# Routed attention with a two-layer feed-forward: two key transfers, the centroids' scaling and their turned copy handed to ScalarE

## The chip, the cores and the metric

The kernel runs on one core of a Trainium2 chip. The metric is the device time of one execution in microseconds (us); lower is better. Each timing below is the median of several executions of the same program.

The core has five engines that work side by side, each through its own list of instructions: TensorE (PE, with weight loads as PEld), VectorE (DVE), ScalarE (ACT), GpSimd (POOL) and SyncE (SP). SP and ACT also issue the DMA transfers of this kernel's prologue; "SPq" and "ACTq" in the profile are such issues.

## What is computed

A routed attention, and a feed-forward behind it. Every query and key is assigned to the centroid to which it is most alike, and a query sees only the keys with the same centroid as itself.

```python
q, k, v: (4, 8, 768, 64)      centroids: (8, 16, 64)
q_n, k_n, c_n = each vector divided by (its norm + 1e-06)
q_assign = argmax over the 16 centroids of q_n . c_n        # k_assign likewise
mask = q_assign[:, :, :, None] == k_assign[:, :, None, :]
scores = where(mask, q k^T / 8, -1e9)
attn = softmax(scores);  x = (attn v), as (3072, 512)
h = x @ w_in                                                # (3072, 2048)
out = (h * erf(softplus(h))) @ w_out                        # (3072, 512)
```

The centroids' scaling `c_n = centroids / (norm + 1e-6)` is the part of this that the change touches; it is done once, for all eight heads.

## The kernel before

The attention works on 16 pairs of heads (`NPAIR`), one after the other. The first two pairs are prepared by straight-line code, the *prologue*; then `period(p, i)` is called six times for each pair and mixes the work of three pairs: the attention of one, the masks of the next and the loads of the one behind it. After the pairs comes the feed-forward (products in banks named `bank`), which is more than half of the time. All of the engines' work up to there is emitted through `InOrder`, a small wrapper that keeps every instruction in the order in which it stands in the program on its engine. So nothing is rescheduled: an instruction that waits holds up all that stand behind it on the same engine.

The prologue, in the order in which the program emits it:

1. **Loads.** `load(p, nm, src, pl)` brings q or k of one pair in four transfers of 96 KB, one for each head `e` of the pair and each half `g` of the 64 features. `queues` holds SP at place 0 and ScalarE at place 1. Of the first pair's q, head 0 goes by SP and head 1 by ScalarE; of its k, `queues[e * g]` sends only the fourth transfer by ScalarE and three by SP. The centroids (32 KB) go by SP ahead of everything. Behind ScalarE's two q transfers stands the load of its function table (`preload_act_table_set`, line 253), and behind that its k transfer. From line 255 on all transfers go by SP: q and k of the second pair (into `x_more`), later those of the third (`load_qk(2)`, line 1498).
2. **Centroids.** Lines 346 to 368. The 128 centroids lie one to a partition in `cen`, a strip of the buffer `pr` (so these steps carry the name `pr` in the profile). VectorE squares and sums them (355, 356), bounds the sum from below (357), ScalarE makes the root through logarithm and exponential (359, 360), VectorE refines it by one Newton step and takes the reciprocal (361 to 367), and then writes the scaled centroids twice side by side into `cn` (368).
3. **Warm-up.** `warm(n, bank, rhs)` (line 1479) issues n matmuls whose results nobody reads: 17 with 256 columns (line 1484), then the one that turns `cn` into the bank `pct` (1486), then 3 with 384 columns (1487). `turned` is the name of both banks in the profile.
4. **Turning.** VectorE turns q into `qT` (1490), copies the two halves of `pct` into `ccT` (1491 to 1495), and turns k into `kT` (1496).
5. **Routing of the first pair.** `similarities(0)`: TensorE multiplies `ccT` with `qT` and `kT`; ScalarE casts `qT` and `kT` to bf16 (`vectors`, tiles `qv` and `kv`); VectorE fills `pick` (lines 1502 to 1509); TensorE does `products(0)` and 9 more warm-up matmuls (1512); `choose(0)` on VectorE turns the similarities (`sims`), takes the maximum (`wide`), compares (`hot`) and turns back (`hotT`). The matmuls of `masks` need `hotT`, and everything after needs the masks.

Of the kernel before, what the change touches and what calls it, by code (L numbers as in the profile page):

```python
# [9 lines left out]
F32 = mybir.dt.float32  # L10
# [5 lines left out]
ACT = mybir.ActivationFunctionType  # L16
# [3 lines left out]
P = 128  # L20
# [115 lines left out]
def kernel(  # L136
# [13 lines left out]
    te, ve, ae, ge = (  # L150
        InOrder(tc, e, in_order) for e in (nc.tensor, nc.vector, nc.scalar, nc.gpsimd)
    )

    def pool(name, bufs, **kw):
        return ctx.enter_context(tc.tile_pool(name=name, bufs=bufs, **kw))

    const = pool("const", 1)
# [3 lines left out]
    turned = [ps.tile([P, 512], F32, name=f"turned{i}") for i in range(2)]  # L161
# [5 lines left out]
    x_more = const.tile([P, 3, HK, HT], F32, name="x_more")  # L167
    minus = const.tile([P, Q], F32, name="minus")
    alleps = const.tile([P, 1], F32, name="alleps")
    x_dram = dram.tile([DM, B * S], F32, name="x_dram")  # L170

    attention = ctx.enter_context(ExitStack())

    def passing(name, bufs, **kw):
        return attention.enter_context(tc.tile_pool(name=name, bufs=bufs, **kw))
# [4 lines left out]
    const = passing("fixed", 1)  # L180
# [8 lines left out]
    pick = const.tile([P, 2, P], BF16, name="pick")  # L189
# [25 lines left out]
    queues = [sy, ae]  # L215

    def heads(p):
        return p // HP, 2 * (p % HP)

    def load(p, nm, src, pl):  # L220
        if p >= NPAIR:
            return
        b, h0 = heads(p)
        if nm == "v":
            t = pl.tile([P, NJ, 2, D], F32, name="in_v")
            for e in range(2):
                queues[0].dma_start(out=t[:, :, e], in_=src[b, h0 + e].rearrange("(j p) d -> p j d", p=P))
        else:

            if pl is None:  # L230
                t = x_more.rearrange("p a k t -> p (a k t)")[:, (nm == "k") * S : (1 + (nm == "k")) * S]
                t = t.rearrange("p (n t) -> p n t", t=Q)
            else:
                t = pl.tile([P, NB, Q], F32, name="in_" + nm)
            for e in range(2):
                for g in range(D // Q):
                    queues[e if nm == "q" else e * g].dma_start(
                        out=t[e * D + g * Q : e * D + (g + 1) * Q],
                        in_=src[b, h0 + e, :, g * Q : (g + 1) * Q].rearrange("(n t) d -> t n d", t=Q),
                    )  # L240
        pairs.setdefault(p, {})[nm] = t

    def load_qk(p):
        load(p, "q", q, stage if p != 1 else None)
        load(p, "k", k, stage if p != 1 else None)
# [3 lines left out]
    cen = setup[:, 0:D]  # L249
    sy.dma_start(out=cen, in_=centroids.rearrange("h c d -> (h c) d"))  # L250

    load(0, "q", q, stage)
    tc.keep_in_program_order(nc.scalar.preload_act_table_set("natural_log_exp_and_others"))
    load(0, "k", k, stage)
# [9 lines left out]
    for base, pattern, sign, op, fill in (  # L264
# [5 lines left out]
            out=first, in_=first, compare_op=op, fill=fill, base=base, pattern=pattern,  # L270
# [69 lines left out]
    ve.tensor_copy(out=identb, in_=ident)  # L340
    ve.memset(minus, -1.0)
    ve.memset(alleps, S * EPS)
    for t in lowest + least:
        ge.memset(t, 0.0)

    cn = setup[:, D : 3 * D].rearrange("p (e d) -> p e d", e=2)
    spare = iter(range(TW, HW))

    def scalar_tile():
        n = next(spare)  # L350
        return setup[:, n : n + 1]

    sq = cn[:, 0]
    ss = scalar_tile()
    ve.tensor_tensor(out=sq, in0=cen, in1=cen, op=ALU.mult)
    ve.reduce_sum(out=ss, in_=sq, axis=AX.X)
    ve.tensor_scalar_max(out=ss, in0=ss, scalar1=1e-30)
    norm = scalar_tile()
    ae.activation(out=norm, in_=ss, func=ACT.Ln)
    ae.activation(out=norm, in_=norm, func=ACT.Exp, scale=0.5)  # L360
    inv = scalar_tile()
    ve.reciprocal(out=inv, in_=norm)
# [2 lines left out]
    norm = scalar_tile()  # L365
    ve.tensor_scalar(out=norm, in0=twice, scalar1=0.5, scalar2=1e-6, op0=ALU.mult, op1=ALU.add)
    rden = scalar_tile()
    ve.reciprocal(out=rden, in_=norm)
    for e in range(2):
        ve.tensor_scalar_mul(out=cn[:, e], in0=cen, scalar1=rden)  # L370

    def transposes(p, which="qk"):

# [1105 lines left out]
    def warm(n, bank, rhs):  # L1479
        for _ in range(n):  # L1480
            te.matmul(bank[:, 0 : rhs.shape[-1]], lhsT=identb, rhs=rhs, start=True, stop=True)

    zeros = lowest[1].rearrange("p t n -> p (t n)")
    warm(17, turned[1], pick.rearrange("p h n -> p (h n)"))
    pct = turned[0][:, 0:P]
    te.transpose(out=pct, in_=cn.rearrange("p e d -> p (e d)"), identity=ident)
    warm(3, turned[1], zeros)
# [1 line left out]
    st["qT"], st["kT"] = rows[0]["q"], rows[0]["k"]  # L1489
    ve.transpose(out=st["qT"], in_=st.pop("q").rearrange("p n t -> p (n t)"))  # L1490
    for e in range(2):
        ve.tensor_copy(
            out=ccT[e * D : (e + 1) * D, :, e * C : (e + 1) * C],
            in_=pct[e * D : (e + 1) * D].rearrange("d (r e c) -> d r e c", e=2, c=C)[:, :, e],
        )
# [6 lines left out]
    for r in (0, D):  # L1502
        for half in range(2):
            for e in range(2):
                c = r + half * Q + e * C
                ve.tensor_copy(
                    out=pick[r : r + D, half, e * D : (e + 1) * D].rearrange("p (n c) -> p n c", n=2)[:, :, 1 : C + 1],
                    in_=first[r : r + D, c : c + C].unsqueeze(1).to_broadcast([D, 2, C]),
# [137 lines left out]
```

## Time and profile before

| | |
|---|---|
| time, median of 3 runs | 950.37 us (950.34 to 950.56) |
| the profiled execution's own time | 950.65 us |
| its span, first to last instruction | 948.9 us |
| TensorE busy | 939.7 us, 99% of the span |
| VectorE, ScalarE, GpSimd busy | 789.1, 546.5, 504.6 us |
| prologue up to the first mask matmul | the first 11.31 us of the span |

A row of the timeline reads: start and duration in us, engine, line, operation, what it writes <- what it reads, shapes, how many instructions are merged in the row, and in brackets how long the engine had been idle before and what it waited for. Since every operation is recorded in the wrapper, nearly all rows name its line, L127; the tiles tell which step it is. In the chain of waits a row is start, duration, engine and what was at work. Matmuls overlap one another, so the time from one start to the next is the better measure of their pace than their durations.

### The profile page before, as it was taken

How to read it: one execution, taken by the hardware profiler on the slowest of the kernel's cores; microseconds unless marked ns; L12 is line 12 of the kernel's file. 1: busy time of each engine (PE TensorE's matmuls, PEld its weight loads, DVE VectorE, ACT ScalarE, POOL GpSimd, SP SyncE). 2: the span in 40 equal slices, each digit the busy share in tenths (PEclk: the TensorE clock that was granted, in tenths of full speed). 3: DMA queues.
4: the chain of work that ended last, by engine and by line, in shares of the span. 5: the costliest groups of instructions: out<-in, count | busy, mean ns of one | idle time of the engine just before them, and what ended most of it. 6: DMA issues, size and time to landing. Idle time of an engine off the chain costs nothing.

```text
span 948.9 us, 22319 instructions
## 1 busy us (share of the span) xinstructions
PE 939.7 (99%) x8756; PEld 707.2 (75%) x8756; DVE 789.1 (83%) x1417; ACT 546.5 (58%) x809; POOL 504.6 (53%) x357
## 2 busy tenths in 40 slices
PE   8999999999999999999999999999999999999998
PEld 3555555555555555588888888998999899989987
DVE  8888888888888887879886688688868977897887
ACT  3677777777777776476523643654257236525541
POOL 1688888888888888899108211360063016103600
PEclk9999999999999999999999999999999999999999
DMA  9344554444443621132876347353444336343433
GB/s 220 69 114 113 112 113 113 111 113 111 113 112 68 156 56 36 26 120 112 220 209 248 111 117 203 123 180 111 157 158 143 133 115 209 113 153 123 156 112 111
DMA packets 176344, 123.17 MB, mean 130 GB/s; under 512 B 132592, under 2 KB 143344, under 8 KB 176240
## 3 DMA queue, kind: packets, MB, share of 16 engines
q1 hardware_dynamic: 171872, 116.34, 42.5%
q0 software_dynamic: 1872, 4.98, 2.9%
q8 instruction: 69, 1.13, 0.5%
q10 hardware_dynamic: 2496, 0.43, 0.2%
q14 instruction: 35, 0.29, 0.1%
HBM read 91.78 MB, written 23.33 MB: 121 GB/s over the span
## 4 chain that ended last, share of the span: by engine, by line
PE 93%; DVE 2%; ACT 2%; issue 1%; POOL 1%; DMA 1%; SPq 0%; DVEq 0%; POOLq 0%; ACTq 0%
PE bank L127 40%; PE turned L127 31%; PE sc L127 16%; PE wide L127 6%; POOL more_out L127 1%; DVE nmx L127 1%; DVE g L127 1%; ACT a_s L127 0%; DMA g_more<-in_moe_w_out_dram 0%; ACT L127 0%; ACT osb L127 0%; ACT w_out L127 0%; SPq L127 0%; DMA qm<-least_rows 0%; ACT g_more L127 0%
## 5 line engine op out<-in xcount | busy, mean ns | idle before, releaser
L127 POOL TENSOR_TENSOR more_out<-more_out,pr 128x768 f32<-128x768 f32 x128 | 217.6, 1700 | 17.1 <-ACT pr L127 7.5
L127 DVE TENSOR_REDUCE nmx<-wide 128x2 f32<-128x512 f32 (+2 forms) x189 | 179.1, 948 | 47.1 <-PE wide L127 46.0
L127 ACT ACTIVATE pr<-sc 128x768 f32<-128x768 f32 x192 | 148.4, 810 | 81.3 <-PE wide L127 73.3
L127 PE MATMUL turned<-pr,in_v 128*32 128x193 f32 x3072 | 145.2, 330 | 0.0
L127 POOL TENSOR_TENSOR g<-g 128x512 f32<-128x512 f32 x36 | 47.1, 1309 | 180.8 <-DVE g L127 178.9
L127 PEld LDWEIGHTS turned<-pr,in_v 128*32 128x32 f32 x3072 | 90.2, 109 | 51.3 <-issue 26.9
L127 DVE TENSOR_TENSOR g<-g 128x512 f32<-128x512 f32 x132 | 90.8, 688 | 22.3 <-PE bank L127 11.8
L127 PE MATMUL sc<-qT,kT 64*128 64x384 f32 x528 | 98.5, 485 | 0.0
L127 DVE TENSOR_TENSOR g<-bank,g 128x256 f32<-128x256 f32 (+1 forms) x128 | 64.7, 531 | 16.1 <-PE bank L127 9.5
L127 PE MATMUL bank<-g_more,g 128*128 128x256 f32 x320 | 75.7, 379 | 0.0
L127 PE MATMUL bank<-x_own,w_in 128*128 128x128 f32 (+1 forms) x440 | 74.0, 310 | 0.0
L127 ACT ACTIVATE a_s<-g 128x1024 f32<-128x1024 f32 x38 | 39.5, 1054 | 57.4 <-POOL g L127 45.6
L127 POOL TENSOR_TENSOR more_out<-pr,pr 128x768 f32<-128x768 f32 x32 | 59.1, 1848 | 20.0 <-ACT pr L127 19.9
L127 DVE TENSOR_TENSOR g<-a_s,g 128x512 f32<-128x512 f32 x76 | 68.2, 916 | 0.9 <-ACT a_s L127 0.9
L127 PEld LDWEIGHTS bank<-g_more,g 128*128 128x128 f32 x320 | 60.7, 190 | 8.6 <-DVE g L127 0.4
L127 PEld LDWEIGHTS bank<-x_own,w_in 128*128 128x128 f32 x440 | 63.1, 191 | 4.6 <-issue 0.6
L127 PE MATMUL wide<-kv,qv 64*128 64x256 bf16 (+2 forms) x378 | 64.8, 327 | 0.9 <-ACT km L127 0.6
L127 PE MATMUL bank<-w_out,g 128*128 128x256 f32 x280 | 64.5, 379 | 0.0
L127 ACT ACT_TABLE_LOAD x40 | 51.3, 1283 | 19.8 <-DVE g L127 19.2
L127 PEld LDWEIGHTS <-qv 64*128 64x128 bf16 x384 | 23.1, 93 | 52.7 <-issue 37.9
L127 PE MATMUL wide<-km,qm 64*128 64x256 bf16 (+4 forms) x378 | 62.2, 326 | 0.0
L127 PEld LDWEIGHTS sc<-qT,kT 64*128 64x128 f32 x528 | 46.3, 187 | 19.0 <-issue 2.0
(240 smaller groups left out, 1992.6 us busy)
## 6 DMA issues: line engine op xcount, KB each, us to landing
g_more<-b_dram SPq DMA_DIRECT2D x52, 512.0 KB
g_more<-w_dram SPq DMA_DIRECT2D x84, 256.0 KB
x_own<-in_moe_w_in_dram SPq DMA_DIRECT2D x13, 512.0 KB
in_v<-in_v_dram SPq DMA_DIRECT2D x32, 192.0 KB
x_dram<-more_out SPq DMA_DIRECT2D x128, 48.0 KB
x_own<-x_dram SPq DMA_DIRECT2D x6, 1024.0 KB
in_k<-in_k_dram SPq DMA_DIRECT2D x59, 96.0 KB
in_q<-in_q_dram SPq DMA_DIRECT2D x58, 96.0 KB
```

The costliest lines, as they stand in the source:

```text
L127: ins = getattr(self.engine, name)(*args, **kw)
```

## The change

- `load` sends both transfers of head 1 by ScalarE for k too, so that SP issues two of the first pair's four k transfers and ScalarE two.
- The instruction that bounds the sum of squares from below is gone; the logarithm takes 1e-30 as a bias from a new tile `tiny`, which VectorE fills once.
- The two scalings into `cn` move from VectorE to ScalarE.
- The first warm-up has 15 matmuls instead of 17.
- The two copies of `pct` into `ccT` move from VectorE to ScalarE. They keep their place in the program, ahead of the casts of `qT` and `kT`.

```diff
+    tiny = const.tile([P, 1], F32, name="tiny")
...
-                    queues[e if nm == "q" else e * g].dma_start(
+                    queues[e].dma_start(
...
     ve.memset(alleps, S * EPS)
+    ve.memset(tiny, 1e-30)
...
-    ve.tensor_scalar_max(out=ss, in0=ss, scalar1=1e-30)
     norm = scalar_tile()
-    ae.activation(out=norm, in_=ss, func=ACT.Ln)
+    ae.activation(out=norm, in_=ss, func=ACT.Ln, bias=tiny)
...
     for e in range(2):
-        ve.tensor_scalar_mul(out=cn[:, e], in0=cen, scalar1=rden)
+        ae.activation(out=cn[:, e], in_=cen, func=ACT.Identity, scale=rden)
...
-    warm(17, turned[1], pick.rearrange("p h n -> p (h n)"))
+    warm(15, turned[1], pick.rearrange("p h n -> p (h n)"))
...
     for e in range(2):
-        ve.tensor_copy(
+        ae.copy(
             out=ccT[e * D : (e + 1) * D, :, e * C : (e + 1) * C],
             in_=pct[e * D : (e + 1) * D].rearrange("d (r e c) -> d r e c", e=2, c=C)[:, :, e],
         )
```

## The prediction

> **What bounds the kernel now.** I read the page's busy times first, then the chain of waits in order of time, then the timelines of the engines over the first 14 us.
>
> ```profile
> span 948.9 us, 22319 instructions
> PE 939.7 (99%) x8756; PEld 707.2 (75%) x8756; DVE 789.1 (83%) x1417; ACT 546.5 (58%) x809; POOL 504.6 (53%) x357
> ```
>
> TensorE is busy nearly throughout, and the change touches no matmul behind the prologue. It can only move the point from which TensorE's unbroken work starts. The chain of waits over the first 40 us, and one row of the chain over the whole span:
>
> ```profile
> 2.41 4.04 PE turned L127 x18
> ...
> 6.70 0.23 DVE ccT L127
> ...
> 6.96 0.99 DVE kT L127
> ...
> 7.99 0.86 PE turned L127 x4
> 8.88 0.59 DVE sims L127
> ...
> 11.31 0.32 PE wide L127
> ```
>
> ```profile
> 404.83 3.59 DMA g_more<-in_moe_w_out_dram
> ```
>
> The prologue hangs on one thread: 18 matmuls (17 warm-ups and the turning of `cn`), the copies into `ccT`, the turning of k, the similarities of k, then VectorE's `sims` to `hotT`, then the mask matmul at 11.31. Whatever is won or lost ahead of `sims` arrives at 11.31 unchanged, if TensorE is free by then, and from there in the end: the one long transfer in the later chain, at 404.83, is issued behind work that moves along. VectorE and ScalarE in detail:
>
> ```profile
> 2.76 0.23 DVE L127 TENSOR_TENSOR pr<-pr 128x64 f32<-128x64 f32 x1 [0.37 <-DMA pr<-in_centroids_dram]
> ...
> 3.28 0.15 DVE L127 TENSOR_SCALAR pr<-pr 128x1 f32<-128x1 f32 x1
> ...
> 4.58 0.16 DVE L127 RECIPROCAL pr<-pr 128x1 f32<-128x1 f32 x1
> 4.78 0.42 DVE L127 TENSOR_SCALAR pr<-pr 128x64 f32<-128x64 f32 x2
> 5.11 0.97 DVE L127 STREAM_TRANSPOSE qT<-in_q 128x768 f32<-128x768 f32 x1
> 6.47 0.46 DVE L127 COPY ccT<-turned 64x64 f32<-64x64 f32 x2 [0.39 <-PE turned L127]
> 6.96 0.98 DVE L127 STREAM_TRANSPOSE kT<-in_k 128x768 f32<-128x768 f32 x1
> 7.86 0.79 DVE L127 COPY pick<-first 64x32 bf16<-64x32 bf16 x8
> ```
>
> ```profile
> 1.83 1.28 ACT L253 ACT_TABLE_LOAD   x1 [1.83 <-issue]
> ...
> 3.47 0.44 ACT L127 ACTIVATE pr<-pr 128x1 f32<-128x1 f32 x2 [0.35 <-DVE pr L127]
> 6.11 0.83 ACT L127 CAST qv<-qT 128x768 bf16<-128x768 f32 x1 [2.21 <-DVE qT L127]
> ...
> 13.38 0.49 ACT L127 ACTIVATE qm<-turned 128x384 bf16<-128x384 f32 x1 [0.63 <-PE turned L127]
> ```
>
> The reader is to see that `kT` stands behind `ccT` on VectorE, starts without a wait as `ccT` ends, and that ScalarE idles 2.21 us before `qv`. With `ccT` on ScalarE, `kT` no longer waits for TensorE; it waits for `qT` and for k to have landed.
>
> **When k lands.** This is the new limit, so it comes first. The issues, and then the packets of SP's queue (q1) in the windows from 0 to 2.4, 4.4, 5.9 and 6.0 us, with ScalarE's (q10) in the first and the last:
>
> ```profile
> 1.86 0.52 ACTq L127 DMA_DIRECT2D in_k<-in_k_dram  x1
> ...
> 2.28 1.98 SPq L127 DMA_DIRECT2D in_k<-in_k_dram  x3
> ...
> 4.30 2.57 SPq L127 DMA_DIRECT2D x_more<-in_q_dram  x4
> ```
>
> ```profile
> q10 hardware_dynamic: 524, 0.07, 17.4%
> q1 hardware_dynamic: 144, 0.03, 6.1%
> ...
> q1 hardware_dynamic: 1737, 0.23, 32.4%
> ...
> q1 hardware_dynamic: 3988, 0.52, 54.9%
> ...
> q1 hardware_dynamic: 4109, 0.53, 55.6%
> q10 hardware_dynamic: 2352, 0.30, 31.5%
> ```
>
> ScalarE's three transfers are 2352 packets, 784 each. SP's centroids are 144, its two q transfers end at 144 + 2 x 784 = 1712, its three k transfers at 144 + 5 x 784 = 4064. So the last packet of k starts where the count passes 4064, between 5.9 and 6.0: 5.96. From the last packet to data that can be used: the centroids' packets had all started by 2.4 and their reader started at 2.76, so the lag is 0.36 or a little more; from above, `kT` found k there at 6.96, so it is at most 1.0. I take 0.5, nearest to the centroids. k is usable at 5.96 + 0.5 = 6.46, with ends at 6.32 and 6.96. The same count for q (1712 by 4.4) gives 4.8 to 4.9.
>
> Does the move of one k transfer shift that? The eight transfers and the centroids are 144 + 8 x 784 = 6416 packets in any split. The two queues together had passed 4109 + 2352 = 6461 by 6.0, and k was the tail of that backlog: SP's third k issue had ended at 2.28 + 1.98 = 4.26, when SP's count had not yet come past q (1712). So issuing earlier doesn't make it land earlier: 5.96 stays. SP's next issue (`x_more`, pair 1's q) comes up by one issue, 1.98 / 3 = 0.66 us, to about 3.6, and could slip between ScalarE's last k packets: at worst a whole transfer, 784 packets at (6461 - 524 - 144) / 3.6 = 1,609 per us (2.4 to 6.0), 0.49 us. I take nothing, since SP still has two k transfers ahead of it in its own queue.
>
> A rule of the Trainium skill, "DMA: Bandwidth & Descriptors", section "Issuing engines are not separate DMA queues", speaks against this part of the change: transfers issued by several engines share the same DMA engines, and spreading them saves only the time of issuing. By that rule too k lands at 6.46 here; by a faith in two queues it would be earlier, the second rival below.
>
> **Part by part.**
>
> *The bound and the bias.* One VectorE instruction of 0.15 goes, and the logarithm moves from 3.47 to 3.28: 0.19 earlier. `tiny` costs one tiny fill before 2.76, in VectorE's 0.37 of idle. The first warm-up waits for the last of these fills (its row below), so it may start 0.04 later.
>
> *ScalarE's second k issue.* 0.52 to 0.66 behind the first, so until 3.0 at the latest or a little after; the table load covers 1.83 to 3.11, the logarithm is wanted at 3.28. Without that cover it would delay the centroids' chain by 0.66 at most.
>
> *Scaling by ScalarE.* The reciprocal ends at 4.74 - 0.19 = 4.55. Two activations of 64 columns: no row shows that size; a 1-column one is 0.44 / 2 = 0.22, a 384-column one 0.49 (`qm`). So `cn` is ready between 5.0 and 5.55; I take 5.05, by the 1-column row. VectorE goes to `qT` as soon as q is there, 4.85 instead of 5.11, until 5.82.
>
> *Two warm-ups fewer.* TensorE's rows:
>
> ```profile
> 2.41 3.81 PE L127 MATMUL turned<-pick,identb 128*128 128x256 bf16 x17 [2.41 <-DVE alleps L127]
> 6.01 0.42 PE L127 MATMUL turned<-ident,pr 128*128 128x128 f32 x1
> 6.22 0.81 PE L127 MATMUL turned<-lowest,identb 128*128 128x384 bf16 x3
> 6.54 0.49 PE L127 MATMUL turned<-lowest,identb 128*128 128x384 bf16 x2
> 8.76 0.92 PE L127 MATMUL sc<-qT,kT 64*128 64x384 f32 x4
> 9.61 1.64 PE L127 MATMUL turned<-lowest,identb 128*128 128x384 bf16 x9
> ```
>
> The turning starts at 6.01, 3.60 after the first of 17: 0.21 each. With 15 it starts at 6.01 - 0.42 + 0.04 = 5.63, and `cn` has 0.1 to 0.6 to spare. It ends at 6.05.
>
> *Copies by ScalarE.* Two at 0.22 to 0.49: `ccT` is there between 6.5 and 7.05. Queued behind them stand the casts `qv` and `kv`; `qv` moves from 6.11 to about 6.5, or 7.05 at worst, and is done before `kT` ends. Nothing reads either before the mask matmul at 11.31. The similarities of q start at 6.6 (7.1 at worst). Those of k can follow about half a us behind, as for the next pair:
>
> ```profile
> 20.77 0.84 PE L127 MATMUL turned<-qT,ccT 128*32 128x384 f32 x4
> ...
> 21.23 0.84 PE L127 MATMUL turned<-kT,ccT 128*32 128x384 f32 x4
> ```
>
> so ccT holds them up to 7.1, at worst 7.6.
>
> *Sum.* `kT` starts at the later of `qT`'s end (5.82) and k (6.46): 6.46 instead of 6.96. The similarities of k start at 7.49 instead of 7.99, `sims` at 8.38 instead of 8.88; the eight `pick` copies end at 8.65 - 0.5 = 8.15, in time. TensorE's `products` and 9 warm-ups follow the similarities, move by the same 0.5 and still end as `hotT` does. The mask matmul comes at 10.81. Gain 0.50 us, ends 0 and 0.64. The profiled execution's 950.65 us (its span of 948.9 and 1.75 around it) would be 950.15; it lies 0.28 over the median of the runs, so on their scale 950.37 - 0.50 = 949.87, say 949.9.
>
> **The rivals.**
>
> 1. *No gain: k lands no sooner than it was read.* If the lag is the full 1.0, or pair 1's q slips between the last k packets, `kT` starts at 6.96 as before: 950.4. For it: no row shows the landing itself. Against: the centroids' lag of 0.36.
>
> 2. *More gain: ScalarE's issue brings k in earlier*, so that `kT` starts right behind `qT` at 5.82. Then `ccT` (6.6 to 7.1) limits the similarities of k to 7.1, 0.9 sooner: 949.5; if `ccT` takes its low end, 949.3. Against: the packet counts, which show a backlog and no late issue.
>
> 3. *The other side: TensorE stays at its slow pace for longer.* The 17 warm-ups come 0.21 apart for 256 columns; the 9 later ones take 0.165 for 384 ((1.64 - 0.32) / 8), so the pace about doubled; the three between show where: the second starts 0.32 after the first, and it and the third fit in 0.49. So it doubled about 6.5, 4.1 us after the first matmul. If `cn` is late, TensorE stands idle between the 15th warm-up and the turning, just before that point; if the doubling then takes another 4.1 us (10.6), the similarities of k end at 7.49 + 2 x 0.86 = 9.2, `products` at 9.2 + 2 x 0.92 = 11.0, and the 9 warm-ups, fast again from there, 9 x 0.165 = 1.5 later, less the overlap of 0.2, at 12.3: the mask matmul at 12.3 instead of 11.31, 1.0 lost: 951.4. It decides from a `cn` later than 5.63, so from activations above 0.5 each. Against: the 384-column row at 0.49, and that the turning and three warm-ups follow directly. The Trainium skill, "TensorE: Matmul & The Clock Gate", section "What's actually happening", has the rule for it: the clock gate opens after a busy window of about 3.4 us, and the window runs freely. This trace's 4.1 us agrees with one such window and its phase; by the rule the next chance would be at about 9.9, not 10.6, and the loss some 0.4 smaller.
>
> 4. *The shift changes later meetings of transfers and waits*, either way, by more than the prologue holds. The chain shows only the one long transfer, so little speaks for it.
>
> **How the numbers follow.** Forecast (949.7 to 950.4 by its ends) 0.53; rival 1, 0.17; rival 2, 0.10; rival 3, 0.12, a third of which is a loss of two such spells (2.0, 952.4); rival 4, 0.08, half to each side. 0.2% of 950.37 is 1.9 us, about what a measurement of this kernel can tell from no change. Forecast, rivals 1 and 2 and most of 3 lie within it: same 0.88. Slower needs the double loss of rival 3 (0.04) or rival 4 (0.04): 0.08; faster only rival 4: 0.04. The range takes in the forecast and the first two rivals, 949.2 to 951.0, and leaves out rivals 3 and 4, 0.20 together.
>
> **What would show it.** `kT` on VectorE near 6.46 with idle before it put down to a transfer of `in_k`: right. `kT` right behind `qT` (5.8): rival 2. `kT` at 6.9 or later: rival 1. The nine warm-ups lasting well over 1.64 and the mask matmul past 11.3: rival 3. ScalarE's `pr` rows for 64 columns of about 0.25 each, done by 5.1, and the turning without idle before it at 5.6, test the middle steps. The forecast is wrong if the mask matmul comes at 10.81 and the time doesn't follow by half a us.

## The result, and the profile after

| | before | changed |
|---|---|---|
| time, median of 22 runs each | 950.38 us (950.06 to 950.93) | 951.88 us (951.43 to 953.5) |
| ratio to before, 95% interval | | 1.0017 [1.0011, 1.0023] |
| span of the profiled execution | 948.9 us | 950.4 us |
| the mask matmul starts at | 11.31 us | 12.77 us |

The change made the kernel 1.5 us slower, where 0.5 faster was forecast, and the time lies outside the range. The loss is complete when the prologue ends (12.77 - 11.31 = 1.46), and the span is longer by the same 1.5. Of the runs below, three fell to a lower granted clock (0.991 to 0.994): 967.72 and 968.23 us stand in no ratio, and 960.58 us, of the kernel with the key transfer back on SP, lifts that kernel's ratio and widens its interval. The chain of waits over the first 14 us of the changed kernel (start, duration, what was at work):

```profile
0.81 2.85 DMA in_q<-in_q_dram
...
3.69 4.71 DMA in_k<-in_k_dram
...
8.41 0.99 DVE kT L127
...
9.45 0.86 PE turned L127 x4
...
10.33 0.59 DVE sims L127
```

Before, TensorE's warm-ups and VectorE stood in the place of the first two rows. Now `kT` waits for k as the prediction said, but k is there at 8.39, where 6.46 was forecast. VectorE, ScalarE and TensorE of the changed kernel:

```profile
2.35 0.06 DVE L127 MEMSET tiny<- 128x1 f32 x1
3.06 0.23 DVE L127 TENSOR_TENSOR pr<-pr 128x64 f32<-128x64 f32 x1 [0.66 <-DMA pr<-in_centroids_dram]
...
6.10 0.98 DVE L127 STREAM_TRANSPOSE qT<-in_q 128x768 f32<-128x768 f32 x1 [0.68 <-DMA in_q<-in_q_dram]
8.41 0.98 DVE L127 STREAM_TRANSPOSE kT<-in_k 128x768 f32<-128x768 f32 x1 [1.33 <-DMA in_k<-in_k_dram]
```

```profile
1.86 2.14 ACTq L127 DMA_DIRECT2D in_k<-in_k_dram  x2
4.05 0.29 ACT L127 ACTIVATE pr<-pr,tiny 128x1 f32<-128x1 f32 x1 [0.94 <-DMA in_q<-in_q_dram]
...
5.45 0.59 ACT L127 ACTIVATE pr<-pr 128x64 f32<-128x64 f32 x2 [0.87 <-DVE pr L127]
6.67 0.43 ACT L127 COPY ccT<-turned 64x64 f32<-64x64 f32 x2 [0.63 <-PE turned L127]
```

```profile
2.41 3.38 PE L127 MATMUL turned<-pick,identb 128*128 128x256 bf16 x15 [2.41 <-DVE tiny L127]
6.18 0.45 PE L127 MATMUL turned<-ident,pr 128*128 128x128 f32 x1 [0.39 <-ACT pr L127]
6.42 1.17 PE L127 MATMUL turned<-lowest,identb 128*128 128x384 bf16 x3
```

Everything that waits for a transfer is late, the centroids too (3.06 for 2.76), and they were issued as before. So it is not a matter of one moved transfer. Two stretches of each kernel, 4 to 6 and 6 to 8 us, before first. A row has the stretch and its length, the busy time of each engine with its number of instructions, then the granted clock, the DMA engines' busy share (it adds up the time of packets that overlap, so it can pass 1) and GB/s:

```profile
4.00:6.00 2.00, 2.00 (x11) 1.44 (x10) 1.86 (x7) 0.00 (x0) 0.00 (x0) 1.00 1.32 204
6.00:8.00 2.00, 1.83 (x12) 0.57 (x10) 1.57 (x7) 0.86 (x2) 0.00 (x0) 1.00 1.04 166
```

```profile
4.00:6.00 2.00, 1.79 (x9) 0.94 (x7) 0.70 (x4) 1.05 (x4) 0.00 (x0) 1.00 1.59 147
6.00:8.00 2.00, 1.82 (x8) 0.67 (x8) 0.98 (x1) 1.29 (x4) 0.00 (x0) 1.00 1.57 152
```

From 4 to 6 us both kernels move pieces of 128 bytes. The changed one has the DMA engines busier (1.59 for 1.32) and moves less (147 GB/s for 204): each packet costs more, by these figures about 22 ns instead of 13.

What differs for every packet of q and k is where it is written. In the memory plan of these programs a tile takes its bytes in each partition of the on-chip memory in steps of 32, in the order of the program: before, `alleps` has 4 bytes at 137472 and the next tile begins at 137504. The new tile `tiny` needs 4 and takes 32, and the tiles behind it move; `x_more` stands ahead of it and stays. Bytes from the start of a partition:

```
            before                      changed
x_more      131200 = 1025 x 128         131200 = 1025 x 128
in_q        208000 = 1625 x 128         208032 = 1625 x 128 + 32
in_k        211072 = 1649 x 128         211104 = 1649 x 128 + 32
in_v        214144 = 1673 x 128         214176 = 1673 x 128 + 32
```

q and k are written in pieces of 128 bytes. Before, each piece filled one block that begins at a multiple of 128; in the changed kernel each lies across two.

The place doesn't slow the pieces from the first one on. GB/s from 3 to 6 us in 40 equal slices, of the changed kernel and then of one of the experiments below, which has all of its edits and q and k at multiples of 128:

```profile
GB/s 210 215 208 200 200 202 181 169 142 148 150 145 147 150 138 152 162 149 152 149 150 152 152 149 147 150 137 154 145 142 152 140 130 142 157 142 142 148 152 135
```

```profile
GB/s 210 207 188 200 197 210 203 191 181 174 176 181 166 196 210 215 215 217 215 212 215 218 217 217 205 212 217 218 218 217 217 218 215 215 217 215 207 210 217 217
```

Until about 3.4 us the changed kernel moves its shifted pieces as fast as the other; then it falls to some 150 and stays there. Why it begins late was not tried.

### The profile page after: what moved, and what is told of

It is laid out like the page before. It is cut to its first block, busy times and chain, and to the rows that moved or that the text cites. A ratio compares the mean times of both kernels' runs of the same rounds, so it can differ in the third digit from the quotient of the medians.

```text
span 950.4 us, 22317 instructions
## 1 busy us (share of the span) xinstructions
PE 939.7 (99%) x8754; PEld 706.9 (74%) x8754; DVE 788.2 (83%) x1413; ACT 548.1 (58%) x813; POOL 505.3 (53%) x357
## 4 chain that ended last, share of the span: by engine, by line
PE 96%; DVE 1%; DMA 1%; POOL 1%; issue 0%; ACT 0%; DVEq 0%; POOLq 0%
PE bank L127 43%; PE turned L127 31%; PE sc L127 16%; PE wide L127 6%; POOL more_out L127 1%; DVE nmx L127 1%; DMA in_k<-in_k_dram 0%; DMA in_q<-in_q_dram 0%; DVE kT L127 0%; ACT qm L127 0%; DVE g L127 0%; ACT pr L127 0%; DVE sims L127 0%; DVE hotT L127 0%; ACT km L127 0%
```

## The experiments

Theory A: the place of the tiles that DMA writes, moved by `tiny`, is the loss. Rival B: the fourth key transfer in ScalarE's queue is. Rival C: the place of other tiles, which the engines read and write, is. All times are medians of 11 runs beside runs of the kernel before on the same chip, which stood at 950.34 to 950.38.

**The 32 bytes alone.** The kernel before, with a tile nobody uses:

```diff
     alleps = const.tile([P, 1], F32, name="alleps")
+    tiny = const.tile([P, 1], F32, name="tiny")
...
+    ve.memset(tiny, 1e-30)
```

> The kernel before, with one more 4-byte tile behind alleps and its fill, and nothing else. The tile takes 32 bytes of each partition, so that in_q, in_k and most tiles behind it begin 32 bytes further, at 32 modulo 64 instead of 0. Theory A (the place of the tiles slows the 128-byte writes of q and k): the first transfers come 0.66 us apart instead of 0.45, k lands near 7.8, kT starts near 7.8 to 8.4 instead of 6.96, the time is 951.3 to 951.9. Rival B (the fourth key transfer in ScalarE's queue is what slows them): kT at 6.96, time 950.4.

951.55 us, ratio 1.0013 [1.0003, 1.0022]. VectorE:

```profile
8.21 0.98 DVE L127 STREAM_TRANSPOSE kT<-in_k 128x768 f32<-128x768 f32 x1 [1.00 <-DMA in_k<-in_k_dram]
```

Of the change's work it has only the fill of `tiny`, and it loses 1.2 of the 1.5. Rival B can't be the main cause.

**The changed kernel, shifted by 64 and by 128 bytes.** All edits are kept; only the width of `tiny` differs, 16 or 32 numbers:

```diff
-    tiny = const.tile([P, 1], F32, name="tiny")
+    tiny = const.tile([P, 16], F32, name="tiny")[:, 0:1]
```

> The changed kernel with tiny made 64 bytes wide, so that in_q begins at 0 modulo 64 again (192 modulo 256), all edits kept. Theory A with a grain of 64 bytes: k lands near 6.5, kT starts there, time 949.9 to 950.1. Theory A with a coarser grain (128 or 256): as the changed kernel, 951.9. Rival B: 951.9.

> The changed kernel with tiny made 128 bytes wide, so that in_q begins at 0 modulo 256, all edits kept. Theory A with any grain up to 256 bytes: kT near 6.5, time 949.9 to 950.1. Rival B: 951.9.

By 64: 951.68, ratio 1.0016 [1.0007, 1.0025], `kT` at 8.24. By 128: 950.16, ratio 0.9998 [0.9989, 1.0006]. VectorE and the same two stretches of the 128-byte shift:

```profile
6.65 0.98 DVE L127 STREAM_TRANSPOSE kT<-in_k 128x768 f32<-128x768 f32 x1 [0.65 <-DMA in_k<-in_k_dram]
```

```profile
4.00:6.00 2.00, 2.00 (x11) 1.30 (x10) 1.67 (x5) 0.59 (x2) 0.00 (x0) 1.00 1.38 215
6.00:8.00 2.00, 2.00 (x10) 0.48 (x9) 1.33 (x6) 1.58 (x4) 0.00 (x0) 1.00 1.18 185
```

With the tiles at a multiple of 128 the rate is back (215 GB/s), and with it `kT` at 6.65. 64 bytes past a multiple of 128 is as slow as 32.

**The key transfer back on SP, the 32 bytes kept.**

```diff
-                    queues[e].dma_start(
+                    queues[e if nm == "q" else e * g].dma_start(
```

> The changed kernel with the key transfer of head 1, half 0 back in SP's queue; tiny and its 32 bytes stay. Theory A: the transfers stay slow and k lands near 7.8, so kT at 7.8 to 8.4; only the logarithm comes earlier (it no longer stands behind a held issue), which is off the path: 951.3 to 951.9. Rival B: the transfers are fast again, kT near 6.5, 949.9.

951.79, ratio 1.0023 [1.0006, 1.0041]; the times alone can't tell it from the changed kernel. `kT` starts at 8.19, 0.22 before the changed kernel's, and the logarithm at 3.32 instead of 4.05:

```profile
1.86 0.52 ACTq L127 DMA_DIRECT2D in_k<-in_k_dram  x1
3.32 0.29 ACT L127 ACTIVATE pr<-pr,tiny 128x1 f32<-128x1 f32 x1 [0.21 <-DVE pr L127]
```

Rival B falls as the cause. Whether the moved transfer is a small loss of its own these two traces can't tell: the centroids, which were issued alike in both, came 0.25 earlier in this one too (2.81 for 3.06).

**Which tiles.** Two runs move the staging tiles, and what lies behind them, apart from the tiles ahead. In the changed kernel 96 unused bytes ahead of `in_q` bring q, k and v back to multiples of 128, while all tiles ahead of them stay shifted; in the kernel before 32 unused bytes there shift q, k, v and what lies behind, and nothing ahead of them (24 and 8 numbers wide; the first is shown):

```diff
     stage = passing("stage", 1)
+    stage_pad = stage.tile([P, 24], F32, name="stage_pad")
...
+    ve.memset(stage_pad[:, 0:1], 0.0)
```

> The changed kernel, tiny and its 32 bytes kept, with 96 unused bytes ahead of in_q, so that in_q, in_k, in_v and what lies behind begin at a multiple of 128 bytes, and all tiles ahead of them (qT, kT, the masks' tiles, pr) stay where the changed kernel has them. Theory A, narrowed (the place of the tiles that DMA writes): k lands near 6.6 and kT starts there, as with the 128-byte shift: 950.1 to 950.3. Rival C (the place of the tiles that the engines read and write is what costs): kT past 8, 951.7 to 951.9.

> The kernel before with 32 unused bytes ahead of in_q (and one small fill of them), so that only in_q, in_k, in_v and what lies behind them begin 32 bytes past a multiple of 128; all tiles ahead keep their places, no edit of the change is in it. Theory A (the place of the tiles that DMA writes): as the shift of all tiles, k lands past 7.5, kT near 8.2, 951.5. Rival C (tiles that the engines alone use also matter): between, 950.6 to 951.2.

950.32, ratio 1.0 [0.9991, 1.001], `kT` at 6.84; and 951.66, ratio 1.0014 [1.0005, 1.0023], `kT` at 8.20. The stretches of the second, from the kernel before but for the 32 bytes:

```profile
4.00:6.00 2.00, 2.00 (x11) 1.45 (x10) 1.16 (x7) 0.00 (x0) 0.00 (x0) 1.00 1.57 150
6.00:8.00 2.00, 1.49 (x9) 0.47 (x8) 1.23 (x3) 0.83 (x1) 0.00 (x0) 1.00 1.56 154
```

The rate falls to 150 GB/s and the whole of the first run's loss is there. So the tiles ahead, `qT`, `kT` and `pr` among them, don't matter, and the place of q, k, v and what lies behind is enough to make the loss and to undo it, but for 0.16 (950.32 for the 950.16 of the 128-byte shift) that lies within the intervals. Of the tiles behind, the prologue's engines use `sims`, `hot` and `hotT`; their rows last as long shifted as not (0.58, 0.55 and 0.58), so rival C falls.

**The edits without the shift.** `tiny` as the second column of `alleps`, within the 32 bytes that are taken already:

```diff
-    alleps = const.tile([P, 1], F32, name="alleps")
-    tiny = const.tile([P, 1], F32, name="tiny")
+    two_small = const.tile([P, 2], F32, name="alleps")
+    alleps, tiny = two_small[:, 0:1], two_small[:, 1:2]
```

> The changed kernel with all its edits, but tiny is the second column of alleps' tile, which lies within the 32 bytes that alleps took already; so no tile moves and in_q begins at 128 modulo 256. Theory A with a grain of 128 bytes: as the 128-byte shift, kT near 6.65, 950.1 to 950.2. A grain of 256 bytes: slow transfers again, 951 or more. The second key issue by ScalarE still stands until a q transfer has landed (near 3.05), so the logarithm starts near 3.4 and not at 3.28.

> As the run without a new tile, and the key transfer of head 1, half 0 back in SP's queue. If moving that transfer to ScalarE's queue is worth nothing or costs a little: k lands near 6.5 and the logarithm starts at 3.28, 949.9 to 950.1, the same or some 0.1 below the run with the transfer on ScalarE. If the move helps: 950.3 or more.

> The run without a new tile and with the key transfer back on SP, and with 17 warm-ups again instead of 15. By the prediction's sum the two warm-ups are off the path once kT waits for k alone: kT at 6.5, mask matmul at 10.95 as with 15, time within 0.15 of that run (949.8 to 950.1). Rival: they were worth their 0.42, the turning of cn, ccT and the similarities come later by that and the mask matmul at 11.1 or later, 950.2 or more.

All edits: 950.18, ratio 0.9998 [0.9989, 1.0007]. Key transfer back on SP: 949.97, ratio 0.9997 [0.9988, 1.0006]. 17 warm-ups as well: 950.12, ratio 0.9998 [0.9989, 1.0007]. `kT` of the three, in that order:

```profile
6.63 0.98 DVE L127 STREAM_TRANSPOSE kT<-in_k 128x768 f32<-128x768 f32 x1 [0.66 <-DMA in_k<-in_k_dram]
```

```profile
6.53 0.98 DVE L127 STREAM_TRANSPOSE kT<-in_k 128x768 f32<-128x768 f32 x1 [0.57 <-DMA in_k<-in_k_dram]
```

```profile
6.54 0.98 DVE L127 STREAM_TRANSPOSE kT<-in_k 128x768 f32<-128x768 f32 x1 [0.60 <-DMA in_k<-in_k_dram]
```

`in_q` lies at 128 modulo 256 here and at 0 in the 128-byte shift, and both have the full rate: a tile need not begin at a multiple of 256. It is not shown that the blocks are of 128 bytes. Where the tiles are shifted by 32 or 64 bytes, every piece lies across a multiple of 128, but every second one lies across a multiple of 256 too; at multiples of 128 none lies across either. With the shift gone, the medians of all three lie below those of before, by 0.16, 0.37 and 0.26; every interval holds 1, so by time alone none is told from no change. The traces show `kT` 0.33 to 0.43 earlier. The version with the key transfer on SP and 15 warm-ups has the lowest median, but the intervals of the three overlap.

**The copies into ccT alone**, on the kernel before:

```diff
-        ve.tensor_copy(
+        ae.copy(
             out=ccT[e * D : (e + 1) * D, :, e * C : (e + 1) * C],
```

> The kernel before with one edit, the two copies into ccT by ScalarE; no tile is added or moved. By the prediction's sum kT then starts when k has landed, 6.5 to 6.55 instead of 6.96, and the mask matmul comes at 10.9 instead of 11.31: 949.9 to 950.0. Rival D (the other edits, the shorter chain of the centroids and the 15 warm-ups, are needed for a gain): kT early but the similarities of q late, mask at 11.2 or later, 950.3.

`kT` starts at 6.58, and the mask matmul at 10.94, 0.37 earlier:

```profile
6.58 0.98 DVE L127 STREAM_TRANSPOSE kT<-in_k 128x768 f32<-128x768 f32 x1 [0.51 <-DMA in_k<-in_k_dram]
```

That is nearly all of what the other versions win there, so this one edit carries the prologue's gain. The time doesn't show it: 950.41, ratio 1.0001 [0.9993, 1.001]. In its trace the lead is lost near 54 us, where ScalarE starts an activation of the attention's scores (`pr<-sc`) at 53.77 after a longer wait, against 53.81 before (its row first, then that of before):

```profile
53.77 0.81 ACT L127 ACTIVATE pr<-sc 128x768 f32<-128x768 f32 x1 [0.97 <-PE turned L127]
```

```profile
53.81 0.81 ACT L127 ACTIVATE pr<-sc 128x768 f32<-128x768 f32 x1 [0.65 <-PE wide L127]
```

In the traces of the three versions without the shift the same row starts at 53.40 to 53.49, after the wait of 0.65 that it has before, so they keep their lead there. Why this one does not was not tried and stays open.

## Why the prediction was wrong

**The step that failed** is the price of `tiny`: "`tiny` costs one tiny fill before 2.76". Its time on VectorE was as said (0.06, in idle time), but its 32 bytes moved the staging tiles, and that costs 1.2 to 1.3 us in the kernel before (the 32 bytes alone, 951.55 for 950.36; from the staging tiles on, 951.66 for 950.38) and 1.7 with all the edits (951.88 for 950.18). It costs more there because `kT` waits for nothing but k: it comes 1.78 later (8.41 for 6.63). In the kernel before `ccT` held it until 6.96 anyway, and it comes 1.25 later (8.21). These 1.7 are most of the 2.0 between forecast and measurement; the other 0.3 is a gain that fell short of 0.5. The sum on k's landing built on it: it counted the packets right, and took their pace from the trace of before as if it belonged to the transfers. It belongs to the tiles' place too. None of the rivals had it.

**The second step that failed** is ScalarE's second key issue, which was to end by 3.0 under the table load. The row of two key issues lasts 2.14, until 4.00, the table load covers it only until 3.11, and the logarithm behind it starts at 4.05, its idle time put down to a q transfer. Without the shift it is shorter but still held (`tiny` is a column of `alleps` there):

```profile
1.86 1.54 ACTq L127 DMA_DIRECT2D in_k<-in_k_dram  x2
3.45 0.29 ACT L127 ACTIVATE pr<-pr,alleps 128x1 f32<-128x1 f32 x1 [0.33 <-DVE pr L127]
```

In the operands of that issue stands a wait for the completion of ScalarE's first q transfer, whose semaphore it takes over. The centroids' chain had 0.1 to 0.6 to spare; with the shift it was late by 0.39 (TensorE's idle time ahead of 6.18). That cost nothing in the end, since `kT` was later still. Moving the key transfer brought nothing: `kT` at 6.63 and 6.65 with it on ScalarE, at 6.53 and 6.54 with it on SP, all four with the tiles at multiples of 128. That is some 0.1 lost, inside the bound of 0.49 that the prediction had set to nothing.

**What was right.** `kT` no longer waits for TensorE but for k. k's landing by the packet count was 6.46 at a lag of 0.5; the runs with the tiles at their old place and the key transfer on SP gave 6.53 and 6.54, a lag of 0.57 to 0.58 if the last packet starts at 5.96 there too. The gain at the mask matmul, forecast as 0.50, is 0.33 to 0.42 in the three runs without the shift. The other terms: two scalings 0.59 (0.44 to 0.98 was the bound), two copies 0.43 (0.44), turning of `cn` at 5.58 in the runs with 15 warm-ups and no shift (5.63). The two warm-ups were off the path: with 17 of them `kT` and the mask matmul (10.89) are as early. The loss, 0.17%, is also within the 0.2% that the prediction counted as the same; but it took 0.2% for about the least that a measurement can tell, and the interval, 0.11% to 0.23% slower, told this loss from none.

**Rival 3** came halfway: `cn` was late, TensorE stood idle for 0.39, and the three warm-ups took 1.17 instead of 0.81, so the pace still was the slow one past 7.0 (the granted clock reads 1.00 in all these stretches; the slow pace shows in the rows alone). There was no price, because the similarities waited for k until 9.45. The clock gate's rule that the prediction drew from the Trainium skill, "TensorE: Matmul & The Clock Gate", section "What's actually happening", has a freely running window. The runs agree: with the same 17 warm-ups at the same start the three behind them took 0.65 in one run and 0.81 in another, so the pace doubled at different times. In the version with the lowest median (15 warm-ups) the similarities of q took 1.24 instead of 0.84 and those of k 0.91, and its mask matmul came 0.06 later than with 17 for that (15 first, then 17):

```profile
6.89 1.24 PE L127 MATMUL turned<-qT,ccT 128*32 128x384 f32 x4
7.56 0.91 PE L127 MATMUL turned<-kT,ccT 128*32 128x384 f32 x4
```

```profile
6.79 0.84 PE L127 MATMUL turned<-qT,ccT 128*32 128x384 f32 x4
7.57 0.84 PE L127 MATMUL turned<-kT,ccT 128*32 128x384 f32 x4
```

## What to carry to other kernels

A new tile, however small, moves all that is laid out behind it. Before costing an added tile by its instructions, ask where the buffers come to lie that transfers fill in small pieces, and keep them where they were (here, for pieces of 128 bytes, at multiples of 128), or put the new values into space that is taken already. When a transfer turns slower without a change of its own, compare the DMA engines' busy share and GB/s of the same stretch: busier engines that move less point to the packets' cost, not to their number.

## What the runs showed of the hardware that was not expected

From 4 to 6 us, while the prologue's transfers by two queues follow one another without a gap, 128-byte pieces written at 32 or 64 bytes past a multiple of 128 move at 147 to 153 GB/s in the five runs that have them, where pieces at a multiple move at 201 to 215 in the seven others. The slow rate is no constant of such pieces. Until about 3.4 us they move at 200 or more, and when SP alone sends the third pair's q to the same shifted tile, from 10.8 to 13 us of the changed kernel, the queue moves 170 GB/s, where before it moved 178 (9.6 to 11.3 us). Whether the extra work is in the memory's write or in the DMA engines was not tried.

The span of the version with all edits and no shift is 0.6 shorter than before's in the profile, though it was 0.33 ahead at the mask matmul. The other 0.28 of the two traces comes at one place in the feed-forward, seen here in TensorE's rows of before and of that version:

```profile
559.14 1.89 PE L127 MATMUL bank<-w_out,g_more 128*128 128x256 f32 x8
561.05 1.99 PE L127 MATMUL bank<-g_more,g 128*128 128x256 f32 x8
562.88 1.46 PE L127 MATMUL bank<-more_out,g 128*128 128x256 f32 x6
```

```profile
558.80 1.89 PE L127 MATMUL bank<-w_out,g_more 128*128 128x256 f32 x8
560.53 1.89 PE L127 MATMUL bank<-g_more,g 128*128 128x256 f32 x8
562.26 1.89 PE L127 MATMUL bank<-more_out,g 128*128 128x256 f32 x8
```

The lead grows from 0.34 to 0.62 there. It is not to be counted as won by the change: the late rows of before (561.05 is 1.91 behind its forerunner, elsewhere it is 1.73) are in the traces of before and of the copies alone, and in none of the ten others, those with the 32 bytes among them. One of the ten comes to that place as late as before does (559.15) and goes through at 1.73. The profiled execution of before also lies 0.28 over the median of its kernel. What delays these two there is open.
